# Moving the rows of two leftover heads into spare rows by small transfers on the SP queue

## The chip, the cores and the metric

One core of a Trainium2 chip runs the kernel. The metric is the device time of one execution in microseconds (us). The engines are named as in the profile: PE (matrix products) and PEld (its weight loads), DVE, ACT and POOL (elementwise work), SP (it only issues transfers here). Transfers run on 16 DMA engines; SP issues them in the order in which they are written, and an issue that waits holds up every later one.

## What is computed

Linear attention with a learned feature map, multiplied by a gated MLP, for 2048 tokens of width 640, in float32:

```python
xn = layernorm(x)
q, k, v = split(xn @ wqkv)                      # 32 heads of 20
phi_q = [softmax(q @ w_phi), softmax(-q @ w_phi)]   # 40 features a head, phi_k alike
o = (phi_q @ (phi_k.T @ v)) / (phi_q @ sum(phi_k) + 1e-6)
s = concat_heads(o) @ wo                        # 640 x 640
g = silu(gelu(xn @ w1 + b1) @ w2 + b2)
out = x + s * g
```

The change touches only the last stage: `phi_q @ (phi_k.T @ v)`, the product with `wo`, and what carries the one to the other.

## The kernel before

Tokens are cut into 16 tiles of 128 and four chunks of 512. The program has three stages: keys, values and queries (to about 258 us), the MLP in twelve units (to about 565 us), and the output stage, which works through the four chunks in the order 2, 3, 0, 1 (`ORDER`). Here they are called block 1 to block 4. From the MLP on the order of every engine, SP included, is the order in which the code is written (`manual_schedule`); nothing reorders it.

For each block `num_groups` makes the attention numerators, transposed. A step is a pair (j, p): p is a half of the block (256 tokens), j a group of heads. `num_t` transposes the scaled features of the group (PE, L736) and copies them to SBUF (`ph`, ACT, L739). `num_m` multiplies them with a block-diagonal matrix made of the key-value sums and splits the result into a high and a low part, so that a float32 product can be made of three fast passes (`PASSES`): ACT writes the high part (L750), DVE the low part (L751). Groups j = 0 to 4 hold six heads each, 120 rows, as two times 60 rows in a tile `oT[0][j]` of 128 rows; the four rows behind each 60 are spare and zero. The matrix for them is `bdk`, and each takes two products (L747). Heads 30 and 31 are left over: j = 5, 40 rows. For them the matrix `bdl` holds the same 40 columns three times, so that one tile, `oT[1]` (in the profile `oTl`), holds high, high and low parts in 120 rows (L754, L756, L757, with the sign column `lowsel`), and `wol` holds the fitting high, low and high parts of the last 40 rows of `wo` (`load_wol`, with `midsel`). So the leftover heads cost one product instead of three.

`finish(c, d, ...)` makes 128 output columns (slice d of 5) of a block: 15 products with `wo_s` and `oT[0]` and one with `wol` and `oT[1]` (L802 to L805). Then DVE multiplies by the gate (L810), POOL adds the input (`xres`, L811), and SP stores the result (L815).

The numerators of a block are made while the block before it is finished: after each of the slices d = 0 to 3 `next(nxt)` does one of four parts, with transposes of four steps and the products of the four steps before (the last part has products only). For block 1 this stands between the products of the last MLP unit, three steps at a time. Beside it `late_q` scales the features of tiles 4 to 7, which blocks 1 and 2 do not need, on POOL (L692, L346) and DVE during blocks 1 and 2, with loads (`eq`, L686) and stores (`phi_dram`, L709) on SP. `load_phi` fetches the features of the block after the next: for block 3 after slice 0 of block 1, for block 4 after slice 3 of block 2.

SP's order around slice d is: load of the input and the gate of slice d + 2 (`load_res`, L785 and L789), store of slice d, what `late_q` issues, and then what `num_groups` issues (nothing, before the change).

Of the kernel before, what the change touches and what calls it, by code (L numbers as in the profile page):

```python
# [45 lines left out]
def hedgehog_gated_mlp_kernel(ctx: ExitStack, tc: tile.TileContext, x, xt_in, wqk, bd, wv, wo, w1, b1, w2, b2, out_t):  # L46
    nc = tc.nc
    const = ctx.enter_context(tc.tile_pool(name="const", bufs=1))
# [31 lines left out]
    def row(shape, dt, name):  # L80
        return rows.tile(shape, dt, tag="R", name=name)
# [32 lines left out]
    lowsel = const.tile([P, 1], F32, name="lowsel")  # L114
    nc.gpsimd.memset(lowsel[:], -1.0)
    nc.gpsimd.affine_select(out=lowsel[:], in_=lowsel[:], pattern=[[0, 1]],
                            compare_op=OP.is_ge, fill=0.0, base=-80, channel_multiplier=1)
    midsel = const.tile([P, 1], F32, name="midsel")
    nc.gpsimd.memset(midsel[:], -1.0)
    nc.gpsimd.affine_select(out=midsel[:], in_=midsel[:], pattern=[[0, 1]],  # L120
                            compare_op=OP.is_ge, fill=0.0, base=-40, channel_multiplier=1)
    nc.gpsimd.affine_select(out=midsel[:], in_=midsel[:], pattern=[[0, 1]],
                            compare_op=OP.is_ge, fill=0.0, base=79, channel_multiplier=-1)
    const.tile([P, 8], F32, name="align")
    bdk = const.tile([P, 10, 64], F32, name="bdk")
    bdl = const.tile([P, 120], F32, name="bdl")


    def load_x(t):
# [442 lines left out]


    def kv_state(kvr):
        nc.gpsimd.memset(bdk[:, :, 60:], 0.0)
        ps = bankB()
        for g, m in enumerate((P, P, 96)):
            nc.tensor.transpose(ps[:120, g * P:g * P + m], kvr[:m, 120 * g:120 * g + 120], ident[:m, :m])
        s3 = ps[:120, :320].rearrange("p (f r) -> p f r", r=32)
        nc.vector.tensor_tensor(bdk[:120, :, :60].rearrange("p f (h d) -> p f h d", d=20),  # L580
                                s3[:, :, None, :20].to_broadcast([120, 10, 3, 20]),
                                mask[:120, None, :, None].to_broadcast([120, 10, 3, 20]), op=OP.mult)
        for r in range(3):
            nc.vector.tensor_tensor(bdl[:80, 40 * r:40 * r + 40].rearrange("p (h d) -> p h d", d=20),
                                    ps[:80, None, 320:340].to_broadcast([80, 2, 20]),
                                    mask[:80, :2, None].to_broadcast([80, 2, 20]), op=OP.mult)
    def kv_norm(kvr):
        zf = slab(F32, "zrep")[:].rearrange("p a b -> p (a b)")
        for e, n in enumerate((360, 360, 320, 240)):
# [118 lines left out]
        yield  # L708
        nc.sync.dma_start(phi_dram[t], ef)  # L709

    def load_wol():
        raw = row([P, D], F32, "raw")
        for r in range(3):
            nc.sync.dma_start(raw[40 * r:40 * r + 40, :], wo[640:680, :])
        wol_h = row([P, D], F32R, "wolh")
        wol = row([P, D], F32R, "wol")
        nc.vector.tensor_copy(wol_h[:120, :], raw[:120, :])
        nc.vector.scalar_tensor_tensor(wol[:120, :], wol_h[:120, :].bitcast(F32), midsel[:120, :], raw[:120, :],
                                       op0=OP.mult, op1=OP.add)
        return wol  # L720


    def load_phi(c):
        tl = [slab(F32R, "phi", (P, 2 * D)) for _ in range(TPC)]
        for i in range(TPC):
# [16 lines left out]
    def num_m(j, oT, p, n, ph):  # L742
        po = bankB()
        sl = slice(256 * p, 256 * p + 256)
        if j < 5:
            for e in range(2):
                nc.tensor.matmul(po[64 * e:64 * e + 64, :256], bdk[:n, 2 * j + e, :], ph[:n, e * 256:(e + 1) * 256],  # L747
                                 start=True, stop=True)
            o2 = oT[0][j]
            nc.scalar.activation(o2[:, 0, sl], po[:, :256], AF.Copy)  # L750
            nc.vector.tensor_tensor(o2[:, 1, sl], po[:, :256], o2[:, 0, sl].bitcast(F32), op=OP.subtract)  # L751
        else:
            for a, b in ((0, 64), (64, 120)):
                nc.tensor.matmul(po[a:b, :256], bdl[:n, a:b], ph[:n, :256], start=True, stop=True)  # L754
            o2 = oT[1]
            nc.scalar.activation(o2[:120, 0, sl], po[:120, :256], AF.Copy)  # L756
            nc.vector.scalar_tensor_tensor(o2[:120, 1, sl], o2[:120, 0, sl].bitcast(F32), lowsel[:120, :],  # L757
                                           po[:120, :256], op0=OP.mult, op1=OP.add)

    def num_groups(phi, oT, size=4):  # L760
        steps = [(j, p) for p in range(2) for j in range(6)]
        before = []
        for k in range(0, 12, size):
            now = [(j, p, *num_t(phi, p, j)) for j, p in steps[k:k + size]]
            for j, p, n, ph in before:
                num_m(j, oT, p, n, ph)
            before = now
            yield
        for j, p, n, ph in before:
            num_m(j, oT, p, n, ph)  # L770
        yield

    def new_oT(home):
# [26 lines left out]
    def finish(c, d, oT, last):  # L800
        ps = bankB()
        steps = [(wo_s[j][:, b, d * P:(d + 1) * P], oT[0][j][:, a, :]) for j in range(5) for a, b in PASSES]  # L802
        steps.append((wol[:120, d * P:(d + 1) * P], oT[1][:120, 1, :]))
        for n, (w, o) in enumerate(steps):
            nc.tensor.matmul(ps[:], w, o, start=n == 0, stop=n == 15)  # L805
        xr, gt = xres.pop((c, d)), gates.pop((c, d))
        for o in range(2):
            sl = slice(o * W2, (o + 1) * W2)
            g = gt[:, sl]
            nc.vector.tensor_tensor(g, ps[:, sl], g, op=OP.mult)  # L810
            (nc.vector if last else nc.gpsimd).tensor_tensor(xr[:, sl], g, xr[:, sl], op=OP.add)  # L811
            if last:
                nc.sync.dma_start(out_t[d * P:(d + 1) * P, c * CW + o * W2:c * CW + (o + 1) * W2], xr[:, sl])
        if not last:
            nc.sync.dma_start(out_t[d * P:(d + 1) * P, c * CW:(c + 1) * CW], xr[:])  # L815
# [18 lines left out]
    for unit in range(units):  # L834
        h, g = divmod(unit, NG)
# [115 lines left out]
        if unit == NG - 1:  # L951
            held = list(ys)
            ys[:] = [None] * KC
    wol = load_wol()
    oT = new_oT(late)
    qe[4] = q_load(4)
    load_res(0)
# [26 lines left out]
    for ci, c in enumerate(ORDER):  # L984
# [15 lines left out]
        if ci + 1 < NCH:  # L1000
            oT = oTn
# [3 lines left out]
def _layout(A_x, A_wqkv, A_w_phi, A_wo, B_w1, B_b1, B_w2, B_b2):  # L1005
# [5 lines left out]
    wo = np.zeros((680, D), a["wo"].dtype)  # L1011
    for k in range(10):
        wo[64 * k:64 * k + 60] = a["wo"][60 * k:60 * k + 60]
    wo[640:] = a["wo"][600:]
# [37 lines left out]
```

## Time and profile before

| | |
|---|---|
| three runs | 697.62, 697.28, 691.02 us; median 697.28 |
| profiled execution | span 688.8 us from first to last instruction; its own time is not listed apart. The span lies 2.2 us under the lowest run and 8.5 us under the median |
| granted clock of PE, mean | 0.996 |
| busy, share of the span | PE 99%, PEld 86%, DVE 66%, POOL 55%, ACT 36% |
| chain that ended last | 96% PE |
| output stage, from 581.4 us | 20 slices in 102.6 us |

A busy PE includes products that are queued and wait: whether PE runs at its pace is read from the spacing of the products, and a wait shows as idle time of PEld. A piece of the chain of work is given with its start, its length and the number of instructions in it, so its length by the number is the spacing.

### The profile page before, as it was taken

To read this page: it belongs to the slowest core of one execution; us is meant where nothing else is said; L and a number is where in the kernel's file an instruction comes from. 1 tells how busy PE (TensorE), PEld (TensorE's weight loads), DVE (VectorE), ACT (ScalarE), POOL (GpSimd) and SP (SyncE) were. 2 spreads that over 40 slices of the span, in tenths; PEclk is the share of its full clock that TensorE was granted. 3 is DMA by queue.
4 is the path that set the end of the run, shared out by engine and by line. 5 is a ranking of instruction groups with operands and counts; after the bars stand their busy time and mean duration, and the time that the engine had idled before them with its cause. 6 is when DMAs were issued, how large, how long until landed. Compare 5 with 4: busy or idle time off the path is not lost.

```text
span 688.8 us, 12182 instructions
## 1 busy us (share of the span) xinstructions
PE 680.1 (99%) x4833; PEld 592.8 (86%) x4833; DVE 453.4 (66%) x730; ACT 251.3 (36%) x398; POOL 376.8 (55%) x336
## 2 busy tenths in 40 slices
PE   8899999999999999999999999999999999999997
PEld 8899999999999998888888888888888887777875
DVE  4688556887667546667978774677977655774232
ACT  3331322332332227343353346632232353425430
POOL 1354344948587455946878853636356640783221
PEclk9999999999999999999999999999999999999999
DMA  9830052824172144328697697276364391886633
GB/s 327 288 104 2 3 149 79 245 68 160 35 212 77 72 145 169 115 69 292 220 328 253 202 429 323 81 272 230 140 218 152 132 391 65 320 292 203 234 92 107
DMA packets 73967, 125.57 MB, mean 182 GB/s; under 512 B 5694, under 2 KB 42686, under 8 KB 73014
## 3 DMA queue, kind: packets, MB, share of 16 engines
q1 hardware_dynamic: 71606, 114.31, 48.8%
q10 hardware_dynamic: 2304, 10.49, 4.3%
q8 instruction: 38, 0.62, 0.4%
q14 instruction: 19, 0.16, 0.1%
HBM read 79.68 MB, written 45.10 MB: 181 GB/s over the span
## 4 chain that ended last, share of the span: by engine, by line
PE 96%; DMA 1%; DVE 1%; issue 1%; POOL 1%; ACT 0%; SPq 0%; POOLq 0%; DVEq 0%
PE pA L307 30%; PE pB L646 24%; PE pB L617 21%; PE pB L805 11%; PE pB L747 3%; PE pA L164 2%; PE pB L736 2%; PE kv L378 2%; DMA folds<-in_wqk_dram 1%; PE pA L293 1%; PE pB L754 1%; PE pB L591 0%; POOL e L328 0%; POOL wv L138 0%; ACT e L333 0%
## 5 line engine op out<-in xcount | busy, mean ns | idle before, releaser
L646 PE MATMUL pB<-hs,w2s 128*128 128x512 f32 x720 | 167.1, 390 | 0.0
L646 PEld LDWEIGHTS pB<-hs,w2s 128*128 128x128 f32 x720 | 134.7, 188 | 29.3 <-PE pB L747 0.8
L617 PE MATMUL pB<-xp,w1s 128*128 128x512 f32 x324 | 81.3, 389 | 0.0
L617 PE MATMUL pB<-xd,w1s 128*128 128x512 f32 x324 | 79.3, 389 | 0.0
L333 ACT ACTIVATE e<-e 128x1280 f32<-128x1280 f32 x32 | 40.7, 1271 | 90.0 <-POOL e L328 90.0
L805 PE MATMUL pB<-oT,wo 128*128 128x512 f32 x300 | 72.9, 395 | 0.0
L655 DVE TENSOR_TENSOR y<-pB,y 128x512 f32<-128x512 f32 x100 | 63.8, 680 | 12.3 <-PE pB L646 12.1
L617 PEld LDWEIGHTS pB<-xd,w1s 128*128 128x128 f32 x324 | 60.8, 188 | 12.6
L617 PEld LDWEIGHTS pB<-xp,w1s 128*128 128x128 f32 x324 | 60.8, 188 | 12.6
L805 PEld LDWEIGHTS pB<-oT,wo 128*128 128x128 f32 x300 | 55.4, 188 | 14.8 <-ACT ph L739 1.2
L346 POOL TENSOR_TENSOR e<-e,rc 128x1280 f32<-128x1280 f32 x16 | 39.0, 2438 | 49.1 <-DVE rc L366 48.8
L346 POOL TENSOR_TENSOR eq<-eq,rc 128x1280 f32<-128x1280 f32 x16 | 37.9, 2370 | 50.2 <-DVE rc L705 50.2
L328 POOL TENSOR_TENSOR e<-nr,e 128x640 f32<-128x640 f32 x32 | 45.5, 1422 | 34.6 <-DVE nr L327 31.7
L307 PE MATMUL pA<-wv,xp 128*128 128x320 f32 x384 | 61.1, 312 | 0.8 <-DVE nr L327 0.4
L307 PE MATMUL pA<-wk,xp 128*128 128x320 f32 x384 | 61.5, 316 | 0.0
L622 ACT ACTIVATE pB<-pB,b1t 128x512 f32<-128x512 f32 x48 | 31.8, 662 | 76.2 <-PE pB L617 26.7
L307 PE MATMUL pA<-wq,xp 128*128 128x320 f32 x384 | 59.0, 309 | 0.0
L307 PEld LDWEIGHTS pA<-wk,xp 128*128 128x128 f32 x384 | 58.3, 193 | 0.2
L307 PEld LDWEIGHTS pA<-wv,xp 128*128 128x128 f32 x384 | 56.9, 188 | 1.7 <-issue 0.7
L307 PEld LDWEIGHTS pA<-wq,xp 128*128 128x128 f32 x384 | 56.9, 188 | 0.1
L692 POOL TENSOR_TENSOR ez<-eq,zrep 128x1280 f32<-128x1280 f32 x16 | 47.3, 2958 | 0.5 <-DMA eq<-e_dram 0.5
L402 POOL TENSOR_TENSOR w1s<-raw,w1s 128x640 fp32r<-128x640 f32 (+1 forms) x18 | 25.7, 1429 | 37.1 <-ACT w1s L401 29.9
(139 smaller groups left out, 1045.2 us busy)
## 6 DMA issues: line engine op xcount, KB each, us to landing
raw<-in_w_dram SPq DMA_DIRECT2D x42, 320.0 KB, 4.4
e_dram<-e ACTq DMA_DIRECT2D x16, 640.0 KB, 4.0
eq<-e_dram SPq DMA_DIRECT2D x16, 640.0 KB, 7.0
phi_dram<-eq SPq DMA_DIRECT2D x16, 640.0 KB, 3.5
phi<-phi_dram SPq DMA_DIRECT2D x16, 640.0 KB, 8.5
xt<-in_x_dram SPq DMA_DIRECT2D x16, 320.0 KB, 4.9
xres<-in_xt_dram SPq DMA_DIRECT2D x20, 256.0 KB, 4.8
out_dram<-xres SPq DMA_DIRECT2D x18, 256.0 KB, 3.0
```

The source lines that it names most:

```text
L307: nc.tensor.matmul(ps[:, hf, :HALF], stat_x(q, o, k, a), ws[k][:, b, hf * HALF:(hf + 1) * HALF], start=n == 0, stop=n == 3 * KC - 1)
L328: nc.gpsimd.tensor_tensor(e5[:, :, :, 1, :], nr[:, :, :, None].to_broadcast([P, 2, 16, DH]), e5[:, :, :, 0, :], op=OP.subtract)
L333: nc.scalar.activation(ef, ef, AF.Exp)
L346: nc.gpsimd.tensor_tensor(e3, e3, rc[:, :, None].to_broadcast([P, 64, DH]), op=OP.mult)
L402: nc.gpsimd.tensor_tensor(sl[:, 1, :n], src, sl[:, 0, :n].bitcast(F32), op=OP.subtract)
L617: nc.tensor.matmul(bank[ch][:], tl[:, a, off + wo_:off + wo_ + P], mov(blk, b), start=new and n == 0, stop=n == len(mms) - 1, skip_group_c ...
L622: nc.scalar.activation(ps, ps, AF.Gelu_apprx_tanh, bias=b1t[:, f:f + 1])
L646: nc.tensor.matmul(ps[:], ws[i][:, b, d * P:(d + 1) * P], hs[o][i][:, a, :], start=i == n == 0, stop=(i, n) == (GF - 1, 2), skip_group_che ...
L655: nc.vector.tensor_tensor(y, ps[:], y, op=OP.add)
L692: nc.gpsimd.tensor_tensor(zv, ef, zf, op=OP.mult)
L747: nc.tensor.matmul(po[64 * e:64 * e + 64, :256], bdk[:n, 2 * j + e, :], ph[:n, e * 256:(e + 1) * 256], start=True, stop=True)
L805: nc.tensor.matmul(ps[:], w, o, start=n == 0, stop=n == 15)
```

## The change

The spare rows are put in another place: each 64 columns of `bdk` are four times 15 columns of numerators and one column of zeros, so every sixteenth row of `oT[0][j]` is spare (rows 15, 31, and so on, eight rows a tile and 40 in all five). The rows of `wo` are laid out to fit on the host, with the 40 rows of the leftover heads in the spare places. `bdl` holds its 40 columns once, and `num_m` makes for j = 5 one product, one ACT copy and one DVE subtraction on 40 rows. A new function `spread` moves eight rows of `oT[1]` (both parts, both halves, 4 KB a row) into the spare rows of tile j, as a transfer on SP. It is issued right behind the second half of each tile, so five times a block and 20 times in all. `load_wol`, `wol`, `lowsel` and `midsel` are gone, and `finish` has 15 products. In `num_groups` the leftover heads come first in each half: j runs 5, 0, 1, 2, 3, 4.

```diff
     def kv_state(kvr):
-        nc.gpsimd.memset(bdk[:, :, 60:], 0.0)
+        nc.gpsimd.memset(bdk[:, :, 15::16], 0.0)
...
-        nc.vector.tensor_tensor(bdk[:120, :, :60].rearrange("p f (h d) -> p f h d", d=20),
-                                s3[:, :, None, :20].to_broadcast([120, 10, 3, 20]),
-                                mask[:120, None, :, None].to_broadcast([120, 10, 3, 20]), op=OP.mult)
-        for r in range(3):
-            nc.vector.tensor_tensor(bdl[:80, 40 * r:40 * r + 40].rearrange("p (h d) -> p h d", d=20),
...
+        for h in range(3):
+            nc.vector.tensor_scalar(
+                bdk[:120].rearrange("p f (q c) -> p f q c", c=16)[:, :, :, 5 * h:5 * h + 5],
+                s3[:, :, :20].rearrange("p f (q i) -> p f q i", i=5), mask[:120, h:h + 1], None, op0=OP.mult)
+        nc.vector.tensor_tensor(bdl[:80].rearrange("p (h d) -> p h d", d=20),
...
-    def load_wol():
-        raw = row([P, D], F32, "raw")
-        for r in range(3):
-            nc.sync.dma_start(raw[40 * r:40 * r + 40, :], wo[640:680, :])
...
         else:
-            for a, b in ((0, 64), (64, 120)):
-                nc.tensor.matmul(po[a:b, :256], bdl[:n, a:b], ph[:n, :256], start=True, stop=True)
+            nc.tensor.matmul(po[:40, :256], bdl[:n, :], ph[:n, :256], start=True, stop=True)
...
+    def spread(j, oT):
+        nc.sync.dma_start(oT[0][j][15::16].bitcast(F32), oT[1][8 * j:8 * j + 8].bitcast(F32))
 
     def num_groups(phi, oT, size=4):
-        steps = [(j, p) for p in range(2) for j in range(6)]
+        steps = [(j, p) for p in range(2) for j in (5, 0, 1, 2, 3, 4)]
         before = []
+
+        def products(group):
+            for j, p, n, ph in group:
+                num_m(j, oT, p, n, ph)
+                if p and j < 5:
+                    spread(j, oT)
...
-        steps.append((wol[:120, d * P:(d + 1) * P], oT[1][:120, 1, :]))
         for n, (w, o) in enumerate(steps):
-            nc.tensor.matmul(ps[:], w, o, start=n == 0, stop=n == 15)
+            nc.tensor.matmul(ps[:], w, o, start=n == 0, stop=n == 14)
```

In the lists of the order below, a row is one instruction or a run of like ones, and "waits" names the engines or the transfers (DMAHW0 to DMAHW7, eight counters that the transfers take in turn) on which it waits; line numbers of the changed kernel are 10 to 21 lower. SP at the end of block 1, before: load and store of slice 3, load of the features of tile 7, load and store of slice 4.

```order
L785 DMA xres<-in_xt_dram 128x512 [waits DMAHW7_49,PE_49,Activation_49]
L789 DMA gt<-g_dram 128x512 [waits DMAHW0_49,DVE_49]
L815 DMA out_dram<-xres 128x512 [waits DMAHW1_49,Pool_49]
L686 DMA eq<-e_dram 128x1280 [waits DMAHW2_49]
L785 DMA xres<-in_xt_dram 128x512 [waits DMAHW3_49,PE_49,Activation_49]
L789 DMA gt<-g_dram 128x512 [waits DMAHW4_49,PE_49]
L815 DMA out_dram<-xres 128x512 [waits DMAHW5_49,Pool_49]
```

The same place after the change:

```order
L770 DMA xres<-in_xt_dram 128x512 [waits DMAHW2_49,PE_49]
L774 DMA gt<-g_dram 128x512 [waits DMAHW3_49]
L799 DMA out_dram<-xres 128x512 [waits DMAHW4_49,Pool_49]
L677 DMA eq<-e_dram 128x1280 [waits DMAHW5_49]
L738 DMA oT<-oTl 8x1024 [waits DMAHW6_49,DVE_49]
L738 DMA oT<-oTl 8x1024 [waits DMAHW7_49,DVE_49]
L738 DMA oT<-oTl 8x1024 [waits DMAHW0_49,DVE_49]
L738 DMA oT<-oTl 8x1024 [waits DMAHW1_49,DVE_49]
L770 DMA xres<-in_xt_dram 128x512 [waits DMAHW2_49,PE_49]
L774 DMA gt<-g_dram 128x512 [waits DMAHW3_49,PE_49]
L799 DMA out_dram<-xres 128x512 [waits DMAHW4_49,Pool_49]
```

Four transfers of leftover rows (tiles 1 to 4) stand behind the store of slice 3, which waits for POOL, and behind a load of 640 KB. PE at the start of block 2, the first seven products of its slice 0, before:

```order
L805 MATMUL pB<-oT,wo 128x512 [waits DVE_49]
L805 MATMUL pB<-oT,wo 128x512 x2
L805 MATMUL pB<-oT,wo 128x512 [waits Activation_49]
L805 MATMUL pB<-oT,wo 128x512
L805 MATMUL pB<-oT,wo 128x512 [waits DVE_49]
L805 MATMUL pB<-oT,wo 128x512 [waits Activation_49]
```

And after:

```order
L789 MATMUL pB<-oT,wo 128x512 [waits DMAHW0_49,DVE_49,Activation_49]
L789 MATMUL pB<-oT,wo 128x512
L789 MATMUL pB<-oT,wo 128x512 [waits DVE_49]
L789 MATMUL pB<-oT,wo 128x512 [waits DMAHW6_49,Activation_49]
L789 MATMUL pB<-oT,wo 128x512
L789 MATMUL pB<-oT,wo 128x512 [waits DVE_49]
L789 MATMUL pB<-oT,wo 128x512 [waits DMAHW7_49,Activation_49]
```

The first product of each tile waits for the transfer into that tile; DMAHW0 is here the transfer into tile 0, DMAHW6 the one into tile 1. SP at the end of slice 3 of block 2, before: load and store of slice 3, then the features of block 4.

```order
L785 DMA xres<-in_xt_dram 128x512 [waits DMAHW4_49,DMAHW1_49]
L815 DMA out_dram<-xres 128x512 [waits DMAHW2_49,Pool_49]
L726 DMA phi<-phi_dram 128x1280 [waits DMAHW3_49]
L726 DMA phi<-phi_dram 128x1280
L726 DMA phi<-phi_dram 128x1280 [waits DMAHW5_49]
L726 DMA phi<-phi_dram 128x1280 [waits DMAHW6_49]
```

And after:

```order
L770 DMA xres<-in_xt_dram 128x512 [waits DMAHW1_49,PE_49]
L799 DMA out_dram<-xres 128x512 [waits DMAHW2_49,Pool_49]
L738 DMA oT<-oTl 8x1024 [waits DMAHW3_49,DVE_49]
L738 DMA oT<-oTl 8x1024 [waits DMAHW4_49,DVE_49]
L738 DMA oT<-oTl 8x1024 [waits DMAHW5_49,DVE_49]
L738 DMA oT<-oTl 8x1024 [waits DMAHW6_49,DVE_49]
L705 DMA phi<-phi_dram 128x1280 [waits DMAHW7_49]
L705 DMA phi<-phi_dram 128x1280 [waits DMAHW0_49]
L705 DMA phi<-phi_dram 128x1280 [waits DMAHW1_49]
L705 DMA phi<-phi_dram 128x1280 [waits DMAHW2_49]
```

The four loads of features now stand behind four transfers that wait for DVE.

More of the change, by code (lines that the diff above doesn't have):

```diff
@@ L113, in hedgehog_gated_mlp_kernel @@
                                 compare_op=OP.is_ge, fill=0.0, base=40 * h + 39, channel_multiplier=-1)
[L114 to L123, printed above, removed]
     const.tile([P, 8], F32, name="align")
     bdk = const.tile([P, 10, 64], F32, name="bdk")
-    bdl = const.tile([P, 120], F32, name="bdl")
+    bdl = const.tile([P, 40], F32, name="bdl")
     def load_x(t):
@@ L709, in q_norm @@
         nc.sync.dma_start(phi_dram[t], ef)
-    def load_wol():
-        raw = row([P, D], F32, "raw")
-        for r in range(3):
-            nc.sync.dma_start(raw[40 * r:40 * r + 40, :], wo[640:680, :])
[L715 to L720, printed above, removed]
     def load_phi(c):
@@ L953, in hedgehog_gated_mlp_kernel @@
             ys[:] = [None] * KC
-    wol = load_wol()
     oT = new_oT(late)
@@ L1010, in _layout @@
     bd = np.zeros((P, 6, 64), a["wphi"].dtype)
[L1011 to L1014, printed above, removed]
+    wo = np.zeros((D, D), a["wo"].dtype)
+    w4 = wo.reshape(10, 4, 16, D)
+    w4[:, :, :15] = a["wo"][:600].reshape(10, 3, 4, 5, D).transpose(0, 2, 1, 3, 4).reshape(10, 4, 15, D)
+    w4[:, :, 15] = a["wo"][600:].reshape(10, 4, D)
     for h in range(H):
```

15 lines of the change are left out of this document (6 added, 9 removed).

## Prediction

> **What bounds the kernel now.** I read the page's first lines and its chain of waits, then the chain of work in order of time from 540 us on, then the timelines of PE, SP, DVE and POOL around the three places where one block hands over to the next, and last the waits of PE and the landing times of the transfers. The head of the page and of its chain:
>
> ```profile
> span 688.8 us, 12182 instructions
> PE 680.1 (99%) x4833; PEld 592.8 (86%) x4833; DVE 453.4 (66%) x730; ACT 251.3 (36%) x398; POOL 376.8 (55%) x336
> PE 96%; DMA 1%; DVE 1%; issue 1%; POOL 1%; ACT 0%; SPq 0%; POOLq 0%; DVEq 0%
> ```
>
> PE carries the chain, so a product taken out of the last stage is worth its spacing, as long as nothing PE waits for comes later than before. The chain of work in that stage (start, length, what) gives the spacings and the moments that I need:
>
> ```profile
> 571.35 0.43 PE pB L754 x4
> 581.56 3.64 PE pB L805 x16
> 605.66 7.51 PE pB L805 x32
> 631.78 1.45 PE pB L747 x12
> 633.66 7.51 PE pB L805 x32
> 641.18 1.39 PE pB L736 x16
> 661.82 22.14 PE pB L805 x96
> ```
>
> An output product takes 22.14 / 96 = 0.231 us; the four instructions of a leftover step (two products, each recorded twice) take 0.43 us. Block 2 starts in the middle of the piece from 605.66, at 609.4. Only one wait of PE for a transfer is in this stage, at the transposes of 641.18:
>
> ```profile
> PEld pB L736 <- DMA phi<-phi_dram: 0.2, 1, 0.2
> ```
>
> **What the change saves on PE.** 20 slices lose one product each: 20 x 0.231 = 4.6 us. Eight leftover steps lose one of two products: 8 x 0.43 / 2 = 1.7 us. The number of transposes and of other products stays. Together 6.3 us, all on the path.
>
> **What costs nothing.** These groups go from DVE (the last column is idle time):
>
> ```profile
> L717 DVE CAST wolh<-raw 120x640 fp32r<-120x640 f32 x1 | 0.5, 498 | 1.9 <-DMA raw<-in_wo_dram 1.9
> L718 DVE SCALAR_TENSOR_TENSOR wol<-wolh,midsel,raw 120x640 fp32r<-120x640 f32 x1 | 2.0, 1971 | 0.1
> L580 DVE TENSOR_TENSOR bdk<-pB,mask 120x600 f32<-120x600 f32 x1 | 0.8, 771 | 0.0
> L584 DVE TENSOR_TENSOR bdl<-pB,mask 80x40 f32<-80x40 f32 x3 | 0.4, 183 | 0.0
> ```
>
> The 2.5 us of `wol` (567.2 to 569.8) lay beside PE's products. In `kv_state` one operation of 0.77 us and three of 0.18 become three of between 0.18 and 0.77 and one of 0.18: from 0.6 less to 1.2 us more on DVE at 434 us, over 130 us ahead of their use; I take zero. The ACT and DVE steps of the leftover heads do as many columns as before; the smaller POOL start-up and the three `wol` loads that go were off the path. `xres` waits for fewer readers of its buffers, which can only help.
>
> **What the transfers cost.** No transfer from SBUF to SBUF is in the trace. The nearest are the smallest ones (KB each, us to landing):
>
> ```profile
> st_dram<-pst SPq DMA_DIRECT2D x4, 2.0 KB, 3.1
> out_dram<-xres SPq DMA_DIRECT2D x4, 128.0 KB, 1.9
> ```
>
> So a transfer of 32 KB alone lands after 1.9 to 3.1 us. Four places have to be gone through.
>
> Into block 1: SP and the transfers are nearly idle, and the last low parts of DVE stand at
>
> ```profile
> 579.57 0.86 DVE L751 TENSOR_TENSOR oT<-pB,oT 128x256 fp32r<-128x256 f32 x2 [0.32 <-ACT oT L750]
> 575.00:587.00 12.00, 12.00 (x78) 8.99 (x77) 6.03 (x12) 4.85 (x12) 1.26 (x2) 1.00 0.01 2
> ```
>
> (the second row is a stretch of time; DMA share 0.01). The two leftover steps ahead bring everything 0.43 us forward. Tile 2 is ready at about 579.8 and lands between 581.8 and 583.0; its first product is due 6 x 0.231 = 1.4 us after the start at 581.1, at 582.5. That is 0 to 0.5 us late; I take 0.2.
>
> Into block 2, the costly one. SP, POOL and DVE there:
>
> ```profile
> 609.58 0.34 SPq L815 DMA_DIRECT2D out_dram<-xres  x1
> 609.97 0.42 SPq L686 DMA_DIRECT2D eq<-e_dram  x1
> 610.50 0.40 SPq L785 DMA_DIRECT2D xres<-in_xt_dram  x1
> 605.23 2.95 POOL L692 TENSOR_TENSOR ez<-eq,zrep 128x1280 f32<-128x1280 f32 x1 [0.55 <-DMA eq<-e_dram]
> 608.12 1.43 POOL L811 TENSOR_TENSOR xres<-gt,xres 128x256 f32<-128x256 f32 x2
> 607.08 1.02 DVE L751 TENSOR_TENSOR oT<-pB,oT 128x256 fp32r<-128x256 f32 x3
> 614.83 1.49 DVE L341 TENSOR_REDUCE rc<-eq 128x64 f32<-128x1280 f32 x1 [2.35 <-DMA eq<-e_dram]
> ```
>
> The store of slice 3 leaves only at 609.58, because POOL is behind: its addition (608.12) stands behind `ez`, which waited for a load. Before the change nothing of block 2 hung on SP. Now the transfers into tiles 1 to 4 stand behind this store and a load of 640 KB; the one into tile 1 takes the place of `xres` at 610.50. This chain starts from the end of slice 0 of block 1, so it moves forward by what PE saved until then, 0.43 + 0.23 = 0.65 us: issue at 609.85. PE meanwhile has saved five products and 0.86 us of leftover steps, 2.0 us, starts block 2 at 607.4 and wants tile 1 three products later, at 608.1. If the transfer lands as if alone, it is there at 609.85 + 1.9 = 611.75 and PE waits 3.7 us. If it lands with the load ahead of it, which came in at 614.83 (DVE waited for it), it is there at 614.2 and PE waits 6.1 us; half a microsecond more if it lands as far behind the load as it is issued. I take 6.1, since the load is the row next to it in the same queue, and keep 3.7 and 6.6. Tiles 2 to 4 follow at 0.4 to 0.5 us each, PE needs them at 0.7 us each: nothing more.
>
> That transfers of a queue keep their order is also what the Trainium skill says in "DMA: Bandwidth & Descriptors", under queues, rings and completion order: on each DMA engine descriptors are consumed in ring order. By that rule the wait is 6.1, without it 3.7 us. No run here shows yet which holds.
>
> Into block 3: the rows that bear on it are
>
> ```profile
> 633.77 0.34 SPq L815 DMA_DIRECT2D out_dram<-xres  x1
> 634.16 2.11 SPq L726 DMA_DIRECT2D phi<-phi_dram  x4
> 632.83 1.29 DVE L751 TENSOR_TENSOR oT<-pB,oT 128x256 fp32r<-128x256 f32 x3 [0.25 <-ACT oT L750]
> 632.33 1.42 POOL L811 TENSOR_TENSOR xres<-gt,xres 128x256 f32<-128x256 f32 x2 [5.38 <-DVE gt L810]
> ```
>
> Counted from the end of slice 3 on PE (631.78), POOL is not behind here: the store goes at +2.0, tile 1 at +2.4, and lands from +4.3 to +5.5; PE wants it at 1.9 for the steps, 15 x 0.231 = 3.5 for slice 4 and 0.7 for tile 0, at +6.1. Hidden. But the four loads of `phi` go four issues later: 4 x 0.39 = 1.6 us (by their own spacing of 0.53, 2.1). PE got their data at +9.4 (641.18), 0.2 late. Now it wants them two products, 0.5 us, sooner, and gets them at +11.0: 0.2 + 0.5 + 1.6 = 2.3 us late. If the landing is set by something else than the issue, 0.7 us stays; with the wider spacing 2.8.
>
> Into block 4: the same order without loads behind; nothing, by the same distances.
>
> **The sum.** -6.3 + 0.2 + 6.1 + 2.3 = +2.3 us. The profiled execution would go from a span of 688.8 to 691.1; on the median, 8.5 us above that span, 697.28 becomes 699.6. With the low ends it is -6.3 + 0 + 3.7 + 0.7 = -1.9 (695.4), with the high ends -6.3 + 0.5 + 6.6 + 2.8 = +3.6 (700.9). So PE does less work and gives the time back in two waits.
>
> **The rivals.**
>
> *The transfers are hidden.* If SP reaches the transfers before PE needs them, or PE's other waits shrink by as much, only the saving stays: 697.28 - 6.3 = 691.0. For it: 20 small transfers, 0.64 MB, and a queue with room at three places. Against it: the store at 609.58 and PE's need at 608.1, read from the same execution; it would need POOL 3 to 4 us sooner there. Half of it (only the wait into block 2 hidden) gives 693.5.
>
> *The clock falls in the wait.* A wait of 6.1 us is longer than any of PE in this trace. What the clock does after thin work is seen early (time, PE busy, ..., the clock is the third number from the right):
>
> ```profile
> 12.00:16.00 4.00, 4.00 (x51) 3.81 (x50) 2.77 (x7) 1.87 (x3) 0.55 (x1) 0.86 1.04 407
> 16.00:20.00 4.00, 4.00 (x23) 3.99 (x23) 1.29 (x2) 0.16 (x1) 0.00 (x0) 0.71 1.03 414
> 24.00:28.00 4.00, 2.70 (x19) 2.26 (x17) 4.00 (x5) 1.33 (x2) 0.97 (x1) 1.00 0.27 68
> ```
>
> The dip cost 4 x (0.14 + 0.29) = 1.7 us; 1.3 us of idle time at 24 to 28 cost none. One such dip behind the wait gives 699.6 + 1.7 = 701.3. The Trainium skill, "TensorE: Matmul & The Clock Gate", part 1, says that the clock is halved after an idle window of about 3.4 us; the trace has no idle time that long and neither bears it out nor speaks against it. By that rule the dip comes with a wait of 6.1 us, and rarely with one of 3.7.
>
> *The transfers land late everywhere* (slower). If a transfer of a few rows takes as long as the loads of features,
>
> ```profile
> phi<-phi_dram SPq DMA_DIRECT2D x16, 640.0 KB, 8.5
> ```
>
> 8.5 us instead of 1.9 to 3.1, all four places wait: 6.1 into block 1, 609.85 + 8.5 - 608.1 = 10.3 into block 2, 2.4 + 8.5 - 6.1 = 4.8 into block 3 (and then `phi` is no longer late) and 4.8 into block 4: 26.0 - 6.3 = +19.7, 717.0. It decides from a landing of 3.7 us on. Against it: 128 KB landed in 1.9.
>
> **How the numbers follow.** Two waits as summed, 0.60; hidden wholly or half, 0.20; the dip on top, 0.12; late everywhere, 0.08. The predicted time is 699.6. The range goes down to the hidden case, 691.0 less half a microsecond, and up past the dip, 701.3, by the 2.7 us that a second dip and the high ends could add, to 704: it leaves the late case out and a little below. A measurement of this kernel can tell about 1% from no change: the three runs themselves lie 1% apart. Faster by over 1% (under 690.3) even the hidden case just misses: 0.06. Slower by over 1% (above 704.3) takes the late case and a little of the dip: 0.10. Within 1%: 0.84.
>
> **What would show it.** Right: 15 products a slice at 0.231 us and eight fewer leftover products; idle time of PEld at the first product of tile 1 in block 2, released by a transfer `oT<-oTl`, of 3.7 to 6.6 us; the store of slice 3 in block 1 as what SP waits for ahead of these transfers; about 2 us at the transposes after slice 0 of block 3, released by `phi`; no wait into block 4. Wrong: no idle time at block 2 (then SP was not held), a wait into block 3 or 4 released by `oT<-oTl` (then landing is longer than 3.1 us), a spacing of products other than 0.231, or a clock under 1.00 outside the start.

## The result and the profile after

| | before | after |
|---|---|---|
| median of seven runs each, us | 695.77 (690.82 to 697.62) | 702.55 (697.61 to 704.87) |
| ratio to before, 95% interval | | 1.0102 [1.0066, 1.0139] |
| profiled execution: own time, span, us | about 690.6, 688.8 | 702.79, 701.0 |
| granted clock of PE, mean | 0.996 | 0.982 |
| output stage (first transposes of features to the end), us | 688.8 - 564.58 = 124.2 | 701.0 - 569.82 = 131.2 |

The changed kernel takes 6.8 us more at the median, 1.0%, though PE does less work. The runs of before are now seven, so its median is 695.77 and not the 697.28 of the first three. Ratios, here and below, are of fast runs; one run of before beside the last experiment took 1724.3 us and is left out of its ratio. The own time of before is its span and the 1.8 us (702.79 - 701.0) that lie around the span in the other execution; the "8.5 us above that span" of the prediction were therefore mostly a difference between executions. The head of the page of after, to be laid beside that of before:

```profile
span 701.0 us, 12146 instructions
PE 684.3 (98%) x4797; PEld 596.2 (85%) x4797; DVE 450.9 (64%) x728; ACT 251.1 (36%) x398; POOL 375.4 (54%) x331
PE 88%; DMA 5%; DVE 4%; issue 1%; POOL 1%; SPq 1%; ACT 1%; DVEq 0%; POOLq 0%
```

PE has 36 records fewer than before, 4797 and not 4833: 20 output products, and two for each of eight leftover products. It is on 88% of the chain that ended last, where it was on 96% before. What took its place are transfers and DVE.

The spans differ by 12.2 us and the medians by 6.8, so ahead of anything else 5 us must be explained that are not the change's. This is the stretch up to 24 us, before and then after (columns: stretch, length, busy time and count of PE, PEld, DVE, ACT, POOL, then granted clock, DMA share, GB/s):

```profile
0.00:24.00 24.00, 22.22 (x200) 21.27 (x200) 11.11 (x24) 8.16 (x12) 4.39 (x24) 0.93 0.94 348
```

```profile
0.00:24.00 24.00, 22.66 (x166) 21.38 (x167) 8.62 (x17) 5.51 (x7) 2.87 (x17) 0.72 0.90 336
```

At a clock of 0.93 these 24 us lose 24 x 0.07 = 1.7 us, at 0.72 they lose 6.7. After gets to the output stage 569.82 - 564.58 = 5.2 us later, and PE's work up to there is the same. So the late start is put down to the clock of the first 24 us, which differs between executions of one kernel as well: the runs of each kernel lie 7 us apart, and the mean clock goes with it in after, 0.980 in the run of 704.87 and 0.989 in that of 697.61. So I compare the output stage alone, from the first transposes, which the chain of work shows here in before and there in after:

```profile
564.58 0.93 PE pB L736 x12
```

```profile
569.82 0.76 PE pB L715 x10
...
621.01 4.43 PE pB L789 x12
...
648.95 5.22 DMA phi<-phi_dram
...
655.69 4.72 PE pB L789 x15
...
675.64 20.64 PE pB L789 x90
```

The stage is 7.0 us longer, which agrees with the 6.8 us of the medians. The last row gives the pace, 20.64 / 90 = 0.229 us a product, as before. In the middle stand the two places that cost: the products of block 2 from tile 1 on (621.01), and the transposes that wait for features in block 3 (done at 655.69). PE's waits for transfers in this stage (total us, times, longest):

```profile
PE pB L789 <- DMA oT<-oTl: 6.8, 1, 6.8
...
PE pB L715 <- DMA phi<-phi_dram: 1.7, 2, 1.3
```

There is no wait into block 1 or block 4 and none for `oT` into block 3. The place of the second on PE's timeline:

```profile
647.80 4.47 PE L789 MATMUL pB<-oT,wo 128*128 128x512 f32 x19
652.66 0.23 PE L715 MATMUL pB<-identr,phi 128*80 128x128 f32 x1 [0.39 <-DMA phi<-phi_dram]
654.21 1.48 PE L715 MATMUL pB<-identr,phi 128*80 128x128 f32 x13 [1.33 <-DMA phi<-phi_dram]
```

The output products end at 652.27, and the 14 transposes are done at 655.69: 3.4 us for what takes 14 x 1.39 / 16 = 1.2 at the pace of the prediction's row of 641.18. Of the 2.2 us lost, 1.7 are the two waits shown; the rest are transposes that run slowly. What held the transfer at block 2 is on the chain and on SP's timeline:

```profile
602.52 8.10 DMA eq<-e_dram
...
610.65 1.50 DVE rc L331
...
612.72 1.00 DVE oT L730 x4
```

```profile
615.05 0.34 SPq L799 DMA_DIRECT2D out_dram<-xres  x1
615.44 0.42 SPq L677 DMA_DIRECT2D eq<-e_dram  x1
615.96 2.56 SPq L738 DMA_DIRECT2D oT<-oTl  x4
...
645.85 2.56 SPq L738 DMA_DIRECT2D oT<-oTl  x4
648.46 2.21 SPq L705 DMA_DIRECT2D phi<-phi_dram  x4
```

Two things made it late. DVE's low parts for block 2 stood behind the feature scaling's sum (L331), which waited until 602.52 + 8.10 = 610.62 for a load; they were ready at 613.7. SP got to the transfers only at 615.96, behind the store that waits for POOL and behind the load. Then the landing took 4.9 us, to 620.87. The load of 640 KB issued at 615.44, just ahead, came in at the same time, as DVE's wait for it shows:

```profile
621.05 1.49 DVE L331 TENSOR_REDUCE rc<-eq 128x64 f32<-128x1280 f32 x1 [3.16 <-DMA eq<-e_dram]
```

And four transfers took SP 2.56 us, 0.64 each, so the feature loads behind them were issued that much later.

Behind each of the two waits PE is slow for a while:

```profile
621.00:625.00 4.00, 3.99 (x11) 3.20 (x12) 2.04 (x2) 0.00 (x0) 2.91 (x1) 0.61 1.04 335
...
654.00:660.00 6.00, 5.79 (x27) 4.93 (x28) 0.00 (x0) 2.49 (x5) 0.27 (x1) 0.72 0.99 330
```

12 products in 4.43 us are 0.369 each, which is 12 x (0.369 - 0.231) = 1.7 us lost; 15 in 4.72 us lose 15 x (0.315 - 0.231) = 1.3.

Last, the leftover step. Before, two steps of ordinary heads and one of leftover heads took 1.06 us (the row below, before) and 0.43 us (the first row of the prediction's chain), 1.49 together. After, the same three steps, at the same place:

```profile
570.29 1.06 PE pB L747 x8
```

```profile
572.28 0.34 PE pB L732
572.62 0.03 PE pB L726
572.65 0.18 PE pB L732
572.84 0.87 PE pB L726 x7
```

That is 0.34 + 0.03 + 0.18 + 0.87 = 1.42 us. Half of the leftover products are gone, and 0.07 us of 0.43.

**The balance of the stage:** 20 output products -20 x 0.231 = -4.6; eight leftover steps at most -8 x 0.07 = -0.6; the wait into block 2 +6.8; its slow products +1.7; the wait for features +2.0 (3.4 - 1.2 = 2.2, and 0.2 was there before); its slow products +1.3. Sum +6.6 of the 7.0 measured.

### The profile page after: what moved, and what is told of

It is laid out like the page before. It is cut to its first block, busy times and chain, and to the rows that moved or that the text cites. A ratio compares the mean times of both kernels' runs of the same rounds, so it can differ in the third digit from the quotient of the medians.

```text
span 701.0 us, 12146 instructions
## 1 busy us (share of the span) xinstructions
PE 684.3 (98%) x4797; PEld 596.2 (85%) x4797; DVE 450.9 (64%) x728; ACT 251.1 (36%) x398; POOL 375.4 (54%) x331
## 4 chain that ended last, share of the span: by engine, by line
PE 88%; DMA 5%; DVE 4%; issue 1%; POOL 1%; SPq 1%; ACT 1%; DVEq 0%; POOLq 0%
PE pA L297 30%; PE pB L637 21%; PE pB L608 19%; PE pB L789 8%; PE pA L154 3%; DMA eq<-e_dram 2%; PE pB L726 2%; PE pB L715 2%; PE kv L368 2%; DVE y L646 1%; DMA folds<-in_wqk_dram 1%; DMA phi<-phi_dram 1%; DMA oT<-oTl 1%; PE pA L283 1%; DVE xhi L662 0%
## 5 line engine op out<-in xcount | busy, mean ns | idle before, releaser
L789 PE MATMUL pB<-oT,wo 128*128 128x512 f32 x300 | 74.8, 405 | 6.8 <-DMA oT<-oTl 6.8
L789 PEld LDWEIGHTS pB<-oT,wo 128*128 128x128 f32 x300 | 57.2, 195 | 22.6 <-issue 7.7
```

The costliest lines, as they stand in the source:

```text
L789: nc.tensor.matmul(ps[:], w, o, start=n == 0, stop=n == 14)
```

## The experiments

The theory to be tested: the saving in output products is real, and is given back in two waits (transfers held on the way into block 2; features loaded behind four more issues) and in the slower clock that each wait brings. The stage times below are made as above, each from one profiled execution; every kernel is the changed one with the edit shown. The last two rows are executions of one program and lie 1.7 us apart, so a difference of about that size between two stage times says little by itself; the rows behind it have to carry it.

| run | stage, us | median, us (runs) | ratio to before, 95% interval |
|---|---|---|---|
| before | 124.2 | 694.71 to 697.47 in the four sets beside the experiments | |
| after | 131.2 | 702.55 (7) | 1.0102 [1.0066, 1.0139] |
| e1_act_queue | 134.3 | 707.71 (4) | 1.0209 [1.0175, 1.0243] |
| e2_no_reader | 124.0 | 695.53 (1) | |
| e3_no_transfers | 120.4 | 691.06 (10) | 0.9946 [0.9914, 0.9978] |
| e4_pair_of_leftovers | 120.8 | 694.01 (1) | |
| e5_filled_waits | 127.5 | 700.69 (1) | |
| e6a_transfers_before_store | 126.3 | 697.79 (1) | |
| e6b_features_earlier | 133.6 | 705.19 (1) | |
| e6_both | 130.3 | 701.44 (4) | 1.0057 [1.004, 1.0074] |
| e7_part_earlier | 122.5 | 693.66 (12) | 0.9941 [0.9906, 0.9975] |
| e7b_part_earlier_store_first | 120.8 | 692.74 (1) | |
| e8_part_earlier_timed | 122.5 | 692.48 (12) | 0.994 [0.9914, 0.9966] |

### The transfers on another queue

```diff
-        nc.sync.dma_start(oT[0][j][15::16].bitcast(F32), oT[1][8 * j:8 * j + 8].bitcast(F32))
+        nc.scalar.dma_start(oT[0][j][15::16].bitcast(F32), oT[1][8 * j:8 * j + 8].bitcast(F32))
```

> Measure: the output stage, from the first transposes of features to the end of the span (124.2 us before the change, 131.2 after). The only edit: the 20 transfers are issued by ACT instead of SP. Theory of the order (PE waits because the transfers stand behind a store that waits for POOL and behind a load of 640 KB, and because the feature loads of block 4 stand behind them): the wait into block 2 falls from 6.9 us to 1 to 3 us, which the late low parts of DVE leave; the wait for features before slice 1 of block 3 falls from 2.3 to under 0.8 us; no clock dip; the stage takes 120 to 122 us. Rival, late landing (a transfer of a few rows is slow by itself): 6 to 7 us of wait stay into block 2 and the stage takes 128 us or more.

The stage went to 134.3 us, not the 120 to 122 of the theory. SP's loads and stores no longer stand ahead of the transfers, and PE's wait for features is gone; but PE now waits for `oT` eight times, at the start of blocks 1, 2 and 3. Its waits, landings from the chain of work (start, us), and ACT's own timeline:

```profile
PE pB L789 <- DMA oT<-oTl: 9.9, 8, 3.9
```

```profile
588.17 2.22 DMA oT<-oTl
...
620.18 5.93 DMA oT<-oTl
...
651.64 5.94 DMA oT<-oTl
```

```profile
617.20 0.57 ACTq L738 DMA_DIRECT2D oT<-oTl  x1
617.81 0.38 ACT L729 ACTIVATE oT<-pB 128x256 fp32r<-128x256 f32 x1 [3.99 <-DVE oT L730]
618.69 0.57 ACTq L738 DMA_DIRECT2D oT<-oTl  x1
```

An issue on ACT waits for DVE's low part of its tile, and ACT's next copy stands behind that issue: the tiles, which were made at DVE's pace, are now made one at a time, 1.49 us apart. That is a new cost of this version. The landing says something about after too. Where the transfer engines were quiet, a transfer landed in 2.2 us; beside the loads of blocks 2 and 3 some took 5.9, in a queue of their own (others less: the one issued at 617.20 was there when PE went on at 620.22, after 3.0 us). The slow one of block 2 landed at 626.11, together with a load of 640 KB that SP had issued 0.6 us ahead of it (DVE waited for that load until 625.94). So a transfer can land as late as a load beside it without standing behind it in one queue. The Trainium skill, "DMA: Bandwidth & Descriptors", under "Issuing engines are not separate DMA queues", says that transfers of all issuing engines run on the same 16 DMA engines and interleave; the 5.9 us agree with it.

### The transfers without a reader

```diff
-        nc.sync.dma_start(oT[0][j][15::16].bitcast(F32), oT[1][8 * j:8 * j + 8].bitcast(F32))
+        nc.sync.dma_start(oT[1][64 + 8 * j:72 + 8 * j].bitcast(F32), oT[1][8 * j:8 * j + 8].bitcast(F32))
```

> The transfers are issued by SP as in the changed kernel, but into rows that nothing reads, so the contribution of heads 30 and 31 to the output is left out. Theory of the order: no wait into block 2, while the feature loads stay behind the transfers: 2.3 us of wait before slice 1 of block 3, with the clock dip of 1.2 us behind it; stage 124.2 - 4.7 + 2.1 + 1.2 = 122.8 us. Rival, transfers cost PE by their traffic or by SP's time alone: a wait into block 2 of some us stays although PE waits for no transfer, stage 126 us or more.

```profile
609.77 7.09 PE L789 MATMUL pB<-oT,wo 128*128 128x512 f32 x30
...
647.00 1.41 PE L715 MATMUL pB<-identr,phi 128*80 128x128 f32 x13 [2.35 <-DMA phi<-phi_dram]
```

124.0 us, 7.2 less than after: the same transfers are issued, at the same places, and with nobody waiting for their data PE goes into block 2 without idle time: the last slice of block 1 and the first of block 2 are one run of 30 products (609.77). The wait for features stays (2.35 us here and 0.51 ahead of it), as it must if it comes from SP's time for issuing. That is more than the 2.3 put down for it, and the slow clock stays with it (0.78 and 0.88 in the two stretches of 5 us from 645 us on), so the stage is 1.2 us over the 122.8 expected. So the cost in block 2 is the wait for their data, and not traffic that they add.

### No transfers

```diff
-                if p and j < 5:
-                    spread(j, oT)
```

> The changed kernel without the transfers (the contribution of heads 30 and 31 is left out): what the taken-out products are worth alone. Theory that a leftover product costs as much as the pair before it, since the two of the pair ran at the same time in different columns of PE: only the output products count, 4.6 us, stage 124.2 - 4.6 + 0.3 = 119.9 us. Rival, the prediction's sum (each leftover product 0.2 us): 6.3 us, stage 118.2 us. No wait over 0.8 us, no clock dip, by both.

120.4 us, 3.8 less than before; by the medians of its set 691.06 - 694.71 = -3.7. This is what the change would be worth if the transfers cost nothing. With the 6.3 us of the prediction the stage would be at 124.2 - 6.3 = 117.9, with the 4.6 us of the output products alone at 119.6, and PE still waits 0.4 us for features where it waited 0.2. The run is on the side of the output products alone, and the next one shows why.

### A second leftover product

No transfers, as in the run before, and one more product of the leftover heads into output rows that nothing reads:

```diff
             nc.tensor.matmul(po[:40, :256], bdl[:n, :], ph[:n, :256], start=True, stop=True)
+            nc.tensor.matmul(po[64:104, :256], bdl[:n, :], ph[:n, :256], start=True, stop=True)
```

> As the kernel without transfers, but the leftover heads take two products again, the second into other columns (its result is not used; heads 30 and 31 are left out as there). Theory of the pair at the same time: eight more products cost nothing, stage as without transfers within 0.3 us, and a leftover step takes about 0.43 us in both. Rival, products one after the other: 1.7 us more.

The three steps of the section on the result, here with both leftover products (L732 and L733):

```profile
573.97 0.34 PE pB L732
574.31 0.01 PE pB L733
574.32 0.21 PE pB L732
574.52 0.01 PE pB L733
574.53 0.86 PE pB L726 x8
```

0.34 + 0.01 + 0.21 + 0.01 + 0.86 = 1.43 us, with one product it was 1.42. The second product costs 0.01 us: two products whose results go to different halves of the output rows (0 to 39 and 64 to 103) run at the same time. The stage is 0.4 us longer than without it, and PE's wait for features 0.5 longer (0.98 and 0.44), so nothing is left for the product. The step in the prediction that priced one of two products at half of 0.43 us was wrong.

### Unread products in the waits

```diff
+    def fill(count, oT):
+        spare = bankB()
+        for _ in range(count):
+            nc.tensor.matmul(spare[:], wo_s[0][:, 0, :P], oT[0][0][:, 0, :], start=True, stop=True)
...
             nc.tensor.matmul(ps[:], w, o, start=n == 0, stop=n == 14)
+            if n == 2 and (c, d) == (ORDER[1], 0):
+                fill(28, oT)
...
             finish(c, d, oT, ci == NCH - 1 and d >= 3)
+            if (ci, d) == (2, 0):
+                fill(9, oT)
```

> The changed kernel with 28 output products more, whose results nobody reads, behind the three products of tile 0 at the start of block 2, and 9 more behind slice 0 of block 3: PE works through most of the two waits instead of standing idle; the transfers are as before. Theory that the clock falls because PE is idle: the waits end when they did, but the products behind them keep 0.231 us instead of 0.369 and 0.315, granted clock 1.00 from 621 us on; stage 131.2 - 1.7 - 1.2 = 128.3 us. Rival, the clock falls for another reason (the transfers, or the products that follow): clock 0.6 to 0.8 behind the waits as before, stage 131 us or more.

The stretch behind the first wait, and PE's products there:

```profile
621.00:625.00 4.00, 4.00 (x20) 3.05 (x20) 2.04 (x2) 0.00 (x0) 3.51 (x2) 1.00 0.94 285
```

```profile
615.61 6.51 PE L788 MATMUL pB<-oT,wo 128*128 128x512 f32 x28
621.99 2.99 PE L794 MATMUL pB<-oT,wo 128*128 128x512 f32 x12
```

37 products more, and the stage is 3.7 us shorter than in after: 127.5. PE is busy without a gap and the clock stays at 1.00 from 570 to 694 us, so behind the second wait too, and the 12 products take 2.99 us in place of 4.43. So the slow products are a cost of the idle time ahead of them, and not of traffic or of the data just moved. The two together were put at 2.9 us; of the other 0.8, 0.4 is at the first place, where the 28 products take 6.4 us (615.61 to 621.99) in place of the wait of 6.8, and the rest isn't resolved in one execution.

### Transfers ahead of the store, features earlier, and both

Three kernels. In the first, for slice 3 of block 1 only, the products of the next block and their transfers come ahead of the store and of the feature scaling (`finish` is given `hold`, and returns the store in place of issuing it):

```diff
-            finish(c, d, oT, ci == NCH - 1 and d >= 3)
+            hold = ci == 0 and d == 3
+            store = finish(c, d, oT, ci == NCH - 1 and d >= 3, hold)
+            if hold:
+                next(nxt, None)
+                store()
             next(lq, None)
...
-            next(nxt, None)
+            if not hold:
+                next(nxt, None)
```

> In block 1 the products of the last part of the numerators, with their transfers, are written ahead of the store of slice 3 and of what the feature scaling issues (load of 640 KB on SP, reduction on DVE); the rest as changed. Theory of the order: the low parts of DVE no longer stand behind the reduction that waits for a load, the transfers leave 5 us earlier, the wait into block 2 falls from 6.9 us to under 2, and the clock dip behind it goes; the wait for features at block 3 stays with its dip. Stage 131.2 - 8.6 + 1.5 = 124.1 us. Rival, late landing: the wait into block 2 stays above 4 us, since the transfers meet the traffic of the block wherever they are issued; stage 127 us or more.

```profile
615.86 4.58 PE L789 MATMUL pB<-oT,wo 128*128 128x512 f32 x12 [1.80 <-DMA oT<-oTl]
```

```profile
615.00:620.00 5.00, 4.14 (x12) 3.27 (x12) 2.18 (x6) 0.00 (x0) 3.78 (x3) 0.67 0.87 251
```

The wait falls from 6.8 to 1.8 us and the stage by 4.9, to 126.3: this order, of SP and DVE together, was the cause of 5.0 of the 6.8. The transfers left about 4 us earlier (at 611.83) and landed in 3.9 us, now ahead of the load of 640 KB. It isn't the 124.1 expected, for the slow products stayed: 12 in 4.58 us, 1.8 lost. This wait of 1.8 us brings the same dip of the clock as the one of 6.8. The Trainium skill, "TensorE: Matmul & The Clock Gate", part 1, puts the half clock behind an idle window of about 3.4 us; here it came behind 1.8, and the measurement decides.

In the second, the features of block 4 are loaded after slice 2 of block 2, ahead of the four transfers:

```diff
-            if ci + 2 < NCH and d == (0 if ci == 0 else 3):
+            if ci + 2 < NCH and d == (0 if ci == 0 else 2):
```

> The four feature loads for block 4 are issued after slice 2 of block 2 instead of after slice 3, so ahead of the store and the four transfers of slice 3. Theory of the order: the wait before slice 1 of block 3 falls from 2.3 us to under 0.8, its dip goes, nothing changes into block 2: 131.2 - 2.1 - 1.2 = 127.9 us. Rival, the transfers now stand behind 2.5 MB of loads, land late, and PE waits 2 to 4 us into block 3 instead: 130 to 132 us.

The stage is worse, 133.6. The features are in time, and now the transfers are late into block 3, behind 2.5 MB of features: PE waits 3.6 us for them there, and still 6.2 into block 2. The third kernel has both edits:

> Both moves together: transfers of block 1 ahead of the store and the load, feature loads a slice earlier. Theory of the order: nearly the stage without transfers (120.4 us), 120.8 to 122 us, so 3 us under the kernel before the change. Rival, late landing: at least one wait of 2 us or more stays at the start of block 2 or 3, stage 124 us or more, no gain over the kernel before.

```profile
649.97 4.90 PE L789 MATMUL pB<-oT,wo 128*128 128x512 f32 x12 [5.30 <-DMA oT<-oTl]
```

```profile
640.97 8.87 DMA oT<-oTl
```

130.3 us against the 120.8 to 122 expected; the rival, that the wait only moves, was right. A 32 KB transfer behind four loads of 640 KB landed after 8.9 us; a wait of 1.9 us into block 2 stays as well. Mending the one wait makes the other, as long as the transfers are issued one slice ahead of their use.

### A part earlier

So the numerators of blocks 2 and 3 are begun one slice earlier: their first part is made ahead of slice 0, the transfers go out after slice 2, and the features of block 4 are loaded behind them.

```diff
+    def ahead(home, tiles):
+        o = new_oT(home)
+        parts = num_groups(tiles, o)
+        next(parts)
+        return o, parts
+
+    oTn, nxt = ahead(slabs, phin)
     for ci, c in enumerate(ORDER):
-        nxt = iter(())
-        if ci + 1 < NCH:
-            oTn = new_oT(late if ci % 2 else slabs)
+        if ci == 2:
+            oTn = new_oT(slabs)
             nxt = num_groups(phin, oTn)
...
-            if ci + 2 < NCH and d == (0 if ci == 0 else 3):
+            if ci + 2 < NCH and d == (0 if ci == 0 else 2):
                 phin = load_phi(ORDER[ci + 2])
...
         if ci + 1 < NCH:
             oT = oTn
+        if ci == 0:
+            oTn, nxt = ahead(late, phin)
```

The first kernel also holds back the store and the feature scaling in slice 2 of block 1 (`hold = ci == 0 and d == 2`):

> The changed kernel with the numerators of blocks 2 and 3 made one slice earlier (their first transposes before slice 0 of the block ahead, the last products behind slice 2), the products of slice 2 of block 1 ahead of its store and of the feature scaling, and the feature loads of block 4 behind the transfers of slice 2 of block 2: the transfers have two slices (7 us) more to land and nothing large ahead of them in SP's order. Theory (order on SP plus 4 to 9 us of landing where loads run beside them): no wait over 1 us into blocks 2 and 3, none over 1 us for features, no clock dip; stage 120.4 to 122 us, 2 to 4 us under the kernel before. Rival (POOL and DVE are so late in block 1 that the low parts and hence the transfers come when they came): a wait of 2 us or more into block 2 stays with a dip, stage 124 us or more.

The second has no such hold:

> The same with store and feature scaling ahead of the products in slice 2 of block 1, as in the changed kernel. Theory: the low parts stand behind the reduction of the feature scaling again and the transfers behind a store and a load; they leave some 5 us later, but have two slices: wait into block 2 between 0 and 2 us; stage up to 124 us.

The third is the second once more, with more runs:

> The same kernel as e7b_part_earlier_store_first, now with enough runs for an interval. Theory (all five waits of PE for transfers and features are gone, the saving of 4.6 us in output products and the 1.8 us of the load that goes stays): the output stage takes 120 to 122 us, 2 to 4 us less than the 124.2 us of before, and the ratio to before lies at 0.993 to 0.997. Rival (the one run of 692.74 was only a start at a good clock): the output stage takes 124 us or more and the ratio lies at 0.998 or above.

In none of the three does PE wait for a transfer of leftover rows or for features. 122.5, 120.8 and 122.5 us, and ratios of 0.994 to before: both timed versions beat before by 2.6 and 3.7 us at the median and after by 9 to 10. The hold isn't needed. Two of the stages lie half a microsecond over the 122 expected; no row shows the 1.8 us that the last expectation names beside the 4.6. One wait, in none of the expectations, is new: within block 2, the transposes for block 3's numerators wait for a low part of the leftover heads on DVE, which is behind the feature scaling. In the last run it is 1.3 us, up to 628.65, and the clock behind it falls:

```profile
628.65 0.52 PE pB L715 x4
...
636.30 1.88 PE pB L726 x16
```

```profile
625.00:632.00 7.00, 5.53 (x35) 3.49 (x33) 5.78 (x15) 2.16 (x4) 4.40 (x4) 0.84 0.69 210
```

It is 0.84 in these 7 us. The first of the three kernels shows the same wait of 1.3 us with a dip behind it (0.75 from 625 to 630 us). In the execution of the last program with 120.8 us the wait is 1.0 us, up to 627.60, and there is no dip:

```profile
627.60 0.51 PE pB L715 x4
...
633.61 1.88 PE pB L726 x16
```

From the end of the wait to the end of the next output products it takes 633.61 - 627.60 = 6.0 us there and 636.30 - 628.65 = 7.7 in the last run. So these slow products account for nearly all of the 1.7 us between the two executions.

A wait of this length does not always bring the dip. In the run with the transfers on ACT a wait of 1.66 us has three products at full pace behind it, and the clock was 1.00 from 616 to 624 us:

```profile
620.22 0.93 PE L789 MATMUL pB<-oT,wo 128*128 128x512 f32 x3 [1.66 <-DMA oT<-oTl]
```

## Why the prediction was right, and where not

The time, 702.55, lies in the range, and the change is at the edge of what was called no change (ratio 1.0102). There is luck in it: counted from the 697.28 of the first three runs, the top of the range, 704, stood for a change of +6.7, and +6.8 came; with more runs before's median fell by 1.5 us. The sum was +2.3 us where the stage shows +7.0: the likeliest case gave the sign and both waits, but not the size. By its steps:

- *Twenty output products less, -4.6*: right. The pace is 0.229, and without transfers the stage is 3.8 us shorter.
- *Eight leftover steps at half of 0.43, -1.7*: wrong by at least 1.1. The four records of a step were two products that ran at the same time; e4 puts the second at 0.01 us. The records were in the trace of before, and their sum divided by two was no measurement of one of them.
- *Into block 1, +0.2*: no wait. All five transfers were issued on quiet engines.
- *Into block 2, +6.1*: right in place, in mechanism and nearly in size, 6.8. With the 5.2 us of the start taken off, PE wanted tile 1 at 621.01 - 6.8 - 5.2 = 609.0 (predicted 608.1) and SP issued its transfer at 615.96 - 5.2 = 610.8 (predicted 609.85): both 0.9 later, of which the leftover steps, which saved next to nothing, explain 0.6 and 0.3; the rest isn't explained. The prediction named only SP's order behind the store; DVE's low parts were held by the same feature scaling, and e6a had to move both to bring 6.8 to 1.8. The landing was 4.9 us, taken as 614.2 - 609.85 = 4.4, and the transfer did come in with the load ahead of it. That their order in one queue is the reason isn't shown: in e1 a transfer came in together with a load of the other queue, after 5.9 us.
- *Features into block 3, +2.3*: 2.2 us late, 0.2 of them there before, which the prediction counted again. Two of its parts were wrong and made up for each other: four issues take 2.56 us and not 1.6, and the features, once issued, were there after 654.21 - 648.46 = 5.8 us, where before they took 7.0 (641.18 - 634.16).
- *Into blocks 3 and 4 for transfers, 0*: right in after. The margin was small, as e6b and e6 show.
- *The clock*: here is the step that failed. A dip behind the wait was set aside as a rival with 0.12, and behind one wait only. There were two, 1.7 and 1.3 us: with the 1.1 of the leftover steps and the 0.7 of the wait into block 2 they are 4.8 us. The two small terms that came out too high take 0.5 of it back, which leaves 4.3 of the 4.7 us by which the sum was short. The only row on idle time was the early stretch in which 1.3 us of it cost nothing; e5 shows that the dips come from the idle time, e6a that 1.8 us can suffice.

The rival "hidden" gave 691.0; e3, with no transfers at all, has that median (691.06), though 3.7 us under its set's before and not 6.3. The rival "late everywhere" did not come: in after, landing was 4.9 us into block 2, and into block 3 it was under 4 (the transfers go from 645.85 on, and PE takes tile 1 at about 649.3 without a wait). Its 6.1 us into block 1 is 5.8 by the prediction's own rows, 579.8 + 8.5 - 582.5.

## What to carry to other kernels

A small transfer that is put between a producer and its reader needs a slice or two of slack, since beside other loads it landed here in 3 to 9 us and not in the 2 of a quiet machine; look at what it is queued behind on the issuing engine, and also at what holds the work that it waits for. When a wait of PE is priced, add the slower products behind it: here every wait of 1.8 us or more had them, at about 2 us each, and shorter ones down to 1.2 us had them or not. And before a product is counted as saved, see whether it ran alone: two products into different halves of the output rows took the time of one.

## What the runs showed of the hardware

- The clock at the start varies from execution to execution: 0.93 in before's profile and 0.72 in after's over the same first 24 us, 5 us of the whole time. Comparing one stage, from the same instruction on, was steadier than comparing spans: in the two executions of the last program the spans (691.0 and 693.7) differ by 2.7 us and the stages by 1.7.
- A PE wait of 1.8 us, and one of 1.3, was followed by several microseconds at a mean clock of 0.67 and 0.84; one of 1.66 (e1), one of 1.0 (e7b) and 1.3 us of idle time near the start (before) were not. So the length of a wait alone doesn't decide it; what does was not tested.
- A transfer of eight rows of 4 KB took SP and ACT 0.57 us to issue (0.64 from one to the next on SP), longer than the 0.42 us of a load of 640 KB.
